# A decode block of attention and ReLU-gated MLP: in thirteen of fifteen steps the products of exponentials and V become a loop of two products per turn, with addresses in registers

## The chip, the cores and the metric

The kernel runs on one core of one Trainium2 chip. The metric is the device time of the program in microseconds (us): the median of 3 runs of the kernel before is 658.72 us (658.65 to 659.09). One further execution was taken by the hardware profiler; it took 658.71 us, of which 656.9 us lie between its first and its last instruction (the span). Times "at" a moment are counted from the start of that span.

## The reference, cut to what matters

One token of each of B = 2 batches passes a pre-norm attention block with a cached K and V, and then a gated MLP. 32 heads of 128 values each attend over 8192 cached positions; K and V together are 268 MB of bfloat16, and each byte is used once.

```python
h = x + _A_ref(_layernorm(x, axis=-1), A_k_cache, A_v_cache, A_wq, A_wo)
h2 = h + _B_ref(_layernorm(h, axis=-1), B_W_gate, B_W_up, B_W_down)
# in _A_ref, for one token (q: 1):
scores = jnp.einsum("bhqd,bhkd->bhqk", q, k) * (Dh ** -0.5)
p = _softmax(scores, axis=-1)
o = jnp.einsum("bhqk,bhkd->bhqd", p, v)
```

## The kernel before, in words

The 64 pairs of batch and head are taken four at a time: fifteen steps of four heads ("quads", i = 0 to 14), and the last quad as two halves. K of a quad is one transfer of 8.39 MB into a tile of 128 partitions by 32768 values: 32 partitions hold one head, and each partition holds 256 positions of 128 values. V of a quad has the same shape. Three such tiles (`bufs`) fill in turn: K of step i uses tile 2i mod 3, and V of step i uses tile 2i+1 mod 3. So V of step i+1 goes where K of step i was, and K of step i+2 goes where V of step i was. `load_tile` (L163 to L170) issues a transfer on SyncE's queue, SP, in one instruction (L168).

One step of the loop at L512 does the following.

- `scores_pe` (L515): the last 24 of the 256 positions of each partition (32 in step 0) go over TensorE. Transposes (L352), copies by ScalarE (L353), products with the query (L343) and some small steps put their scores into `scol`.
- `products` (L517, at L378) and `scores` (L523, at L396 and L398): VectorE multiplies the other 232 positions with the query and adds them up by halving. A last reduction (L402) gives the largest score of each partition.
- `largest_of_own` and `place_own` (L530, L533): a largest value is found for each head, ScalarE takes the exponentials (L418), and VectorE lays them out (L423) in `pgq`, the stationary operand of what follows: 64 blocks of 16 columns, one block for 4 positions.
- `values` (L443 to L454): 64 products on TensorE, one per block, each 128 x 16 against 128 x 512 of V, all added up in one bank of PSUM (`pv_ps`). They are 64 instruction pairs (load of weights, matmul) written out one after the other, with addresses fixed in the instructions. ScalarE copies the sum out (L454) to `pv`, to the rows that belong to the quad. In PSUM the sum stands on those same rows.
- After steps 3, 7 and 11 (and 14) the quads that are done are normalised together. So steps 4, 8 and 12 issue their first 8 products, then a small product for the sums (`sums`), and then the other 56.

Nothing here is ordered by a planner. The block at L190 (`tc.manual_schedule()`) keeps the order of the source on every engine, and semaphores are put in where one instruction needs another's result or its tile. A transfer stands in SP's queue where its `load_tile` stands in the source. In a step, V of the next step is asked for after `scores` (L527), and K of the step after next comes behind `values` (L547). Steps 12 and 13 deviate a little (L525, L542, L549, L551), because the last quad is split in two. What follows the loop (step 14, the two halves, the output projection and the MLP) is written out in the same manner.

Of the kernel before, what the change touches and what calls it, by code (L numbers as in the profile page):

```python
# [7 lines left out]
ACT = mybir.ActivationFunctionType  # L8
# [15 lines left out]
def kernel(  # L24
# [13 lines left out]
    nc = tc.nc  # L38
    P = nc.NUM_PARTITIONS
    B, Sq, D = A_x.shape  # L40
    _, Hkv, Sk, Dh = A_k_cache.shape
# [13 lines left out]
    HALF = TILE // 2  # L55
    TPC = 8
    VG = 4


    NPE = 32  # L60
# [37 lines left out]
    qpair = consts.tile([P, 2, Dh], bf16)  # L98
    pgq = consts.tile([P, TILE // Dh // VG, NH, VG], bf16)
    pgp = consts.tile([P, 2, HALF // Dh // VG, 2, VG], bf16)  # L100
    pv = consts.tile([P, VG * Dh], f32)
    pick = consts.tile([P, VG, 4, NH], f32)
    zc = consts.tile([P, B, NQ, NH], f32)
# [56 lines left out]
    steps = [Step(i) for i in range(LASTQ + 3)]  # L160
    Q = LASTQ

    def load_tile(cache, s, dst, pieces=1):  # L163
        h = NH * s.g + (0 if s.quad else 2 * s.k)
        n = s.nt * Dh
        w = n // pieces
        for k in range(pieces):
            nc.sync.dma_start(  # L168
                out=dst[:, k * w:(k + 1) * w], in_=_dram(cache, (s.b * Hkv + h) * Sk * Dh + k * w, [[n, P], [1, w]]),
            )  # L170
# [16 lines left out]
        nc.vector.reciprocal(out=rstd, in_=rstd)  # L187
        nc.vector.tensor_tensor(out=dst_bkc, in0=dev, in1=_free(rstd, 0, [[1, B], [0, KC]]), op=ALU.mult)

    with tc.manual_schedule():  # L190

        for b, k, n in ((0, 0, KC), (1, 0, KC)):
            nc.scalar.dma_start(
                out=xr[b:b + 1, k * P:(k + n) * P], in_=_dram(A_x, b * D + k * P, [[D, 1], [1, n * P]]),
# [10 lines left out]
            out=nscale, in_=nscale, compare_op=ALU.not_equal, fill=-SCALE,  # L205
# [5 lines left out]
            out=ident_f, in_=ident_f, compare_op=ALU.not_equal, fill=1.0,  # L211
# [4 lines left out]
            out=sel, in_=sel, compare_op=ALU.not_equal, fill=1.0,  # L216
# [9 lines left out]
            out=pick, in_=pick, compare_op=ALU.not_equal, fill=1.0,  # L226
# [24 lines left out]
        for g0 in range(0, NQ, 4):  # L251
            for n0 in range(NH * g0 * Dh, NH * (g0 + 4) * Dh, 4 * Dh):
                q_ps = ps2.tile([B, 4 * Dh], f32, tag="o")
                for c in range(KC):
                    nc.tensor.matmul(  # L255
                        out=q_ps, lhsT=xn[:, c, :], rhs=wq_sb[:, c, n0:n0 + 4 * Dh], start=(c == 0), stop=(c == KC - 1),
                    )
                nc.vector.tensor_copy(qrow[:, n0:n0 + 4 * Dh], q_ps)  # L258
            for b in range(B):
                r_ps = ps2.tile([P, 4, Dh], f32, tag="tp")  # L260
                for j in range(NH):
                    nc.tensor.matmul(
                        out=r_ps[j * (P // NH):(j + 1) * (P // NH)], lhsT=sel[:, b, 0:P // NH],
                        rhs=_free(qrow, (NH * g0 + j) * Dh, [[NH * Dh, 4], [1, Dh]]), start=True, stop=True,
# [4 lines left out]
        for j in range(2):  # L269
            nc.tensor.matmul(  # L270
                out=r_ps[j * (P // 2):(j + 1) * (P // 2)], lhsT=sel[:, B - 1, :],
                rhs=_free(qrow, (Hq - NH + j) * Dh, [[2 * Dh, 2], [1, Dh]]), start=True, stop=True,
            )
        nc.scalar.activation(out=qpair, in_=r_ps, func=ACT.Copy)
        for b in range(B):
# [3 lines left out]
            nc.vector.tensor_copy(  # L279
                qTs[:, b].rearrange("p (g j) -> p g j", j=NH), _free(qT_ps, 0, [[P, NQ], [P // NH, NH]]),  # L280
            )
        load_tile(A_k_cache, steps[1], steps[1].kt)

        nc.gpsimd.tensor_copy(
            qzp[:, :, 6:8], qTs[:, B - 1, Hq - NH:Hq].rearrange("p (k j) -> p k j", j=2),
        )
# [42 lines left out]
        def scores_pe(s, between=lambda: None):  # L329


            U = s.npe // 4
            nh, nv = s.nh, s.nv
            row_ps = ps.tile([nh * U, 4 * P], f32, tag="row")

            def times_q(c0):
                for k in range(0, TPC, 4):
                    u = (c0 + k) // 4
                    if s.quad:
                        z = qz[:, QZ - NH - NH * u:QZ - NH - NH * u + NH * U]  # L340
                    else:
                        z = qzp[:, s.k, 6 - 2 * u:6 - 2 * u + 2 * U]
                    nc.tensor.matmul(  # L343
                        out=row_ps, lhsT=z, rhs=s.kt[:, (nv + c0 + k) * Dh:(nv + c0 + k + 4) * Dh],
                        start=(u == 0), stop=(u == U - 1),
                    )

            for c0 in range(0, s.npe, TPC):
                t_ps = ps2.tile([P, TPC, P], bf16, tag="tp")
                for k in range(TPC):  # L350
                    t = nv + c0 + k
                    nc.tensor.transpose(t_ps[:, k, :], s.kt[:, t * Dh:(t + 1) * Dh], ident)  # L352
                nc.scalar.activation(  # L353
                    out=s.kt[:, (nv + c0) * Dh:(nv + c0 + TPC) * Dh], in_=t_ps.rearrange("p t s -> p (t s)"), func=ACT.Copy,
                )
                between()
                if c0:
                    times_q(c0 - TPC)
            times_q(s.npe - TPC)
            rows = s.kt[0:nh * U, nv * Dh:nv * Dh + 8 * P].bitcast(f32)  # L360
            nc.scalar.activation(out=rows, in_=row_ps, func=ACT.Copy)  # L361
            between()
            sc_ps = ps.tile([P, 4, U, nh], f32, tag="row", name="sc_ps")
            for t in range(4):
                nc.tensor.transpose(  # L365
                    sc_ps[:, t].rearrange("p u j -> p (u j)"), rows[:, t * P:(t + 1) * P], ident_f[0:nh * U, 0:nh * U],
                )
            for j in range(nh):
                r = s.rows(j)
                nc.scalar.activation(  # L370
                    out=scols[s.i][r, nv:s.nt].rearrange("p (u t) -> p t u", t=4), in_=sc_ps[r, :, :, j], func=ACT.Copy,
                )
# [67 lines left out]

        pv_ps = {}

        def values(s, u0, u1):  # L443

            r = slice(32 * (s.g % 4), 32 * (s.g % 4) + s.nh * VG)
            if u0 == 0:
                pv_ps[s.i] = ps2.tile([P, VG * Dh], f32, tag="o", name="pv_ps")
            for u in range(u0, u1):
                nc.tensor.matmul(  # L449
                    out=pv_ps[s.i][r, :], lhsT=s.pg[:, u].rearrange("p j t -> p (j t)"),  # L450
                    rhs=s.vt[:, u * VG * Dh:(u + 1) * VG * Dh], start=(u == 0), stop=(u == s.nt // VG - 1),
                )
            if u1 == s.nt // VG:
                nc.scalar.activation(out=pv[r, :], in_=pv_ps[s.i][r, :], func=ACT.Copy)  # L454

        def diagonals(i):

# [54 lines left out]
        for i in range(Q):  # L512
            s = steps[i]
            scols[i] = small.tile([P, s.nt], f32, tag="scol", name="scol")
            scores_pe(s)  # L515
            place_q(steps[i + 1])
            products(s)  # L517
            if i - 2 in groups:
                shares(i - 2)
                normalise(i - 2)  # L520
            if i == Q - 1:
                lay_rows(0, [spread(0, b) for b in range(B)], scalar=True)
            scores(s)  # L523
            if i == Q - 2:
                load_tile(A_k_cache, steps[Q], steps[Q].kt)  # L525
            else:
                load_tile(A_v_cache, steps[i + 1], steps[i + 1].vt)  # L527
            if i == Q - 1:
                scores_pe(steps[Q])
            largest_of_own(s)  # L530
            if i == Q - 1:
                products(steps[Q], 0, NEXT)
            place_own(s)  # L533
            half = s.nt // VG // 2
            ahead = 8 if i - 1 in groups else 0
            if ahead:
                own_sums(i - 1)
                values(s, 0, ahead)
                sums(i - 1)
            values(s, ahead, half)  # L540
            if i == Q - 1:
                load_tile(A_k_cache, steps[Q + 1], steps[Q + 1].kt)  # L542
            values(s, half, 2 * half)
            if i in groups:
                diagonals(i)
            if i + 2 < Q:
                load_tile(A_k_cache, steps[i + 2], steps[i + 2].kt)  # L547
            elif i == Q - 2:
                load_tile(A_v_cache, steps[Q - 1], steps[Q - 1].vt)  # L549
            else:  # L550
                load_tile(A_k_cache, steps[Q + 2], steps[Q + 2].kt)  # L551


        s, p0, p1 = steps[Q:]
# [16 lines left out]
        at = [0, 0]  # L571
# [28 lines left out]
        turns = iter((first, second, third))  # L600
# [3 lines left out]
        for w, src in ((0, B_W_gate), (1, B_W_up)):  # L604
            nc.sync.dma_start(
                out=wgu[:, w].rearrange("p c f -> p (c f)"), in_=_dram(src, 0, [[KC * F, P], [1, KC * F]]),
# [4 lines left out]
        f0, n = FSETS[-2]  # L611
        for d0 in range(0, D, D // 2):
            nc.sync.dma_start(
                out=wd_sb[:, f0 // P:f0 // P + n, d0:d0 + D // 2],
                in_=_dram(B_W_down, f0 * D + d0, [[n * D, P], [D, n], [1, D // 2]]),
# [9 lines left out]
            out=z2_ps, lhsT=ones, rhs=_free(zc, ((B - 1) * NQ + groups[Q][1]) * NH, [[1, nb]]), start=True, stop=True,  # L625
# [11 lines left out]
            out=parts3, in0=ident[0:PARTS, HI:HI + B], in1=ident[0:PARTS, LOW:LOW + B], op=ALU.add,  # L637
# [3 lines left out]
        half = p1.nt // 2  # L641
# [53 lines left out]
        for c in range(KC):  # L695
            nc.tensor.transpose(hT_ps[:, c, :], hb[:, c], ident)
        nc.scalar.activation(
            out=hrow.rearrange("q (p c) -> q p c", c=KC), in_=hT_ps.rearrange("q c p -> q p c"), func=ACT.Copy,
# [3 lines left out]
            out=shift, in0=_free(g_ps, ONE, [[ONE + 1, FC], [0, B]]), in1=_free(mean, 0, [[0, FC], [1, B]]), op=ALU.mult,  # L702
# [3 lines left out]
            out=gate, in_=_free(g_ps, 0, [[ONE + 1, FC], [1, B], [B, 2]]), axis=AXIS.X, op=ALU.add,  # L706
# [7 lines left out]
            out=gate, in0=gate, scalar=0.0, in1=_free(rvar, 0, [[0, FC], [1, B]]), op0=ALU.max, op1=ALU.mult,  # L714
# [63 lines left out]
```

## Time and profile before

| what | value |
|---|---|
| median of 3 runs | 658.72 us (658.65 to 659.09) |
| the profiled execution | 658.71 us; its span 656.9 us, so 1.8 us lie around the span |
| mean granted TensorE clock | 0.761 of full speed |
| VectorE busy | 557.1 us, 85% of the span |
| TensorE matmuls busy | 348.8 us, 53% |
| ScalarE busy | 123.6 us, 19% |
| products with V (L449), 960 in steps 0 to 14 | 239.7 us busy in sum |
| read from memory | 281.09 MB, 428 GB/s over the span |

An engine's busy time is the time in which the hardware profiler saw it work. Work on a semaphore, a branch or a register is not in it, and neither is the issuing of a transfer. A line of a group gives the busy time, the mean duration of one instruction, then the idle time before these instructions with what ended most of it. Matmuls are pipelined, so the mean duration of one (415 ns for L449) is longer than the distance between two (239.7 us by 960 is 250 ns). The chain of waits is followed back from the last instruction, at each step to what released it. In all views SPq is the queue of SP.

### The profile page before, as it was taken

To read this page: it belongs to the slowest core of one execution; us is meant where nothing else is said; L and a number is where in the kernel's file an instruction comes from. 1 tells how busy PE (TensorE), PEld (TensorE's weight loads), DVE (VectorE), ACT (ScalarE), POOL (GpSimd) and SP (SyncE) were. 2 spreads that over 40 slices of the span, in tenths; PEclk is the share of its full clock that TensorE was granted. 3 is DMA by queue.
4 is the path that set the end of the run, shared out by engine and by line. 5 is a ranking of instruction groups with operands and counts; after the bars stand their busy time and mean duration, and the time that the engine had idled before them with its cause. 6 is when DMAs were issued, how large, how long until landed. Compare 5 with 4: busy or idle time off the path is not lost.

```text
span 656.9 us, 5097 instructions
## 1 busy us (share of the span) xinstructions
PE 348.8 (53%) x2116; PEld 157.9 (24%) x2116; DVE 557.1 (85%) x248; ACT 123.6 (19%) x337; POOL 9.1 (1%) x37
## 2 busy tenths in 40 slices
PE   2530924709175380926538092562909458291997
PEld 1210311304022130312214031220403224130456
DVE  1399697988979799897979989797997969999982
ACT  1130030300203030030302103030210304201870
POOL 3000000000000000000000000000000000000020
PEclk9875876958778695877959588695957869576895
DMA  9999999999999999999999999999999999999997
GB/s 383 447 444 443 391 448 439 447 443 397 447 439 432 447 408 447 431 435 436 423 447 424 435 440 427 443 420 439 443 423 440 419 448 435 423 440 408 430 428 296
DMA packets 6766, 281.40 MB, mean 428 GB/s; under 512 B 724, under 2 KB 1368, under 8 KB 1624
## 3 DMA queue, kind: packets, MB, share of 16 engines
q1 hardware_dynamic: 6740, 281.09, 99.1%
q8 instruction: 16, 0.26, 0.1%
q14 instruction: 6, 0.05, 0.0%
q10 hardware_dynamic: 4, 0.00, 0.0%
HBM read 281.09 MB, written 0.00 MB: 428 GB/s over the span
## 4 chain that ended last, share of the span: by engine, by line
DVE 42%; DMA 40%; PE 16%; ACT 1%; issue 1%; SPq 0%; DVEq 0%; ACTq 0%
DMA tile<-in_A_k_cache_dram 31%; DVE tile L378 19%; DVE tile L396 18%; PE pv_ps L449 15%; DMA tile<-in_B_W_down_dram 4%; DMA tile<-in_A_wo_dram 4%; DVE scol L398 2%; DMA tile<-in_A_wq_dram 2%; PE q_ps L255 2%; DVE pgq L423 1%; ACT ecol L418 1%; DVE pm L402 0%; DVE qrep L398 0%; DVE pm L413 0%; DVE hmax L415 0%
## 5 line engine op out<-in xcount | busy, mean ns | idle before, releaser
L449 PE MATMUL pv_ps<-tile,pgq 128*16 128x512 bf16 x960 | 239.7, 415 | 239.9 <-DVE pgq L423 227.8
L378 DVE TENSOR_TENSOR tile<-tile,qrep 128x29696 bf16<-128x29696 bf16 (+3 forms) x16 | 232.4, 14524 | 49.0 <-DMA tile<-in_A_k_cache_dram 49.0
L396 DVE TENSOR_TENSOR tile<-tile 128x14848 bf16<-128x14848 bf16 (+7 forms) x68 | 236.4, 3477 | 2.2
L449 PEld LDWEIGHTS <-pgq 128*16 128x16 bf16 x960 | 90.7, 96 | 378.6 <-DVE pgq L423 238.5
L353 ACT ACTIVATE tile<-t_ps 128x1024 bf16<-128x1024 bf16 x53 | 52.6, 1022 | 17.4 <-PE t_ps L352 16.9
L454 ACT ACTIVATE pv<-pv_ps 16x512 f32<-16x512 f32 (+1 forms) x16 | 9.4, 588 | 238.9 <-PE pv_ps L449 238.8
L418 ACT ACTIVATE ecol<-scol,nmax 128x256 bf16<-128x256 f32 x14 | 7.1, 508 | 200.1 <-DVE nmax L417 200.1
L352 PE MATMUL t_ps<-ident,tile 128*128 128x128 bf16 x424 | 32.0, 227 | 17.5 <-DMA tile<-in_A_k_cache_dram 17.5
L343 PE MATMUL row_ps<-tile,qz 128*24 128x512 bf16 (+1 forms) x98 | 30.9, 398 | 17.9 <-ACT tile L353 17.8
L352 PEld LDWEIGHTS <-tile 128*128 128x128 bf16 x424 | 25.4, 102 | 32.7 <-DMA tile<-in_A_k_cache_dram 18.2
L398 DVE TENSOR_REDUCE scol<-tile 128x232 f32<-128x1856 bf16 (+1 forms) x14 | 28.9, 2067 | 0.5
L423 DVE TENSOR_TENSOR pgq<-ecol,ownb 128x1024 bf16<-128x1024 bf16 x15 | 10.4, 691 | 10.3 <-ACT ecol L418 10.3
L384 ACT ACTIVATE tile<-tile 128x128 bf16<-128x128 bf16 x60 | 17.6, 294 | 1.9 <-DVE tile L378 1.9
L378 DVE TENSOR_TENSOR tile<-tile,qpair 128x4096 bf16<-128x4096 bf16 (+3 forms) x4 | 15.5, 3881 | 0.0
L343 PEld LDWEIGHTS <-qz 128*24 128x24 bf16 (+1 forms) x98 | 7.9, 92 | 27.8 <-issue 22.7
L365 PE MATMUL sc_ps<-ident_f,tile 24*128 24x24 f32 (+2 forms) x68 | 7.4, 224 | 11.0 <-ACT tile L361 11.0
L370 ACT ACTIVATE scol<-sc_ps 32x24 f32<-32x24 f32 (+1 forms) x56 | 11.7, 209 | 7.7 <-PE sc_ps L365 7.2
L361 ACT ACTIVATE tile<-row_ps 24x512 f32<-24x512 f32 (+2 forms) x17 | 9.9, 585 | 14.0 <-PE row_ps L343 14.0
L258 DVE CAST tile<-q_ps 2x512 bf16<-2x512 f32 x8 | 5.4, 679 | 7.2 <-PE q_ps L255 7.2
L255 PE MATMUL q_ps<-tile,xn 128*2 128x512 bf16 x32 | 10.0, 477 | 2.5 <-DMA tile<-in_A_wq_dram 2.5
L384 ACT ACTIVATION_READ_ACCUMULATOR tile<-tile 128x1 f32 x60 | 11.2, 187 | 0.0
L365 PEld LDWEIGHTS sc_ps<-ident_f,tile 24*128 24x128 f32 (+2 forms) x68 | 5.6, 141 | 19.8 <-ACT tile L361 19.8
(135 smaller groups left out, 124.9 us busy)
## 6 DMA issues: line engine op xcount, KB each, us to landing
tile<-in_A_k_cache_dram SPq DMA_DIRECT2D x2, 4096.0 KB, 19.1
tile<-in_A_v_cache_dram SPq DMA_DIRECT2D x2, 4096.0 KB, 20.5
tile<-in_A_wq_dram SPq DMA_DIRECT2D x1, 4096.0 KB, 12.2
tile<-in_A_wo_dram SPq DMA_DIRECT2D x1, 2048.0 KB, 24.1
tile<-in_A_wo_dram SPq DMA_DIRECT2D x2, 1024.0 KB, 23.4
tile<-in_B_W_gate_dram SPq DMA_DIRECT2D x1, 1376.0 KB
tile<-in_B_W_up_dram SPq DMA_DIRECT2D x1, 1376.0 KB, 26.8
tile<-in_B_W_down_dram SPq DMA_DIRECT2D x1, 640.0 KB, 27.7
```

What stands on the lines that cost most here:

```text
L255: nc.tensor.matmul(out=q_ps, lhsT=xn[:, c, :], rhs=wq_sb[:, c, n0:n0 + 4 * Dh], start=(c == 0), stop=(c == KC - 1),)
L343: nc.tensor.matmul(out=row_ps, lhsT=z, rhs=s.kt[:, (nv + c0 + k) * Dh:(nv + c0 + k + 4) * Dh], start=(u == 0), stop=(u == U - 1),)
L352: nc.tensor.transpose(t_ps[:, k, :], s.kt[:, t * Dh:(t + 1) * Dh], ident)
L353: nc.scalar.activation(out=s.kt[:, (nv + c0) * Dh:(nv + c0 + TPC) * Dh], in_=t_ps.rearrange("p t s -> p (t s)"), func=ACT.Copy,)
L365: nc.tensor.transpose(sc_ps[:, t].rearrange("p u j -> p (u j)"), rows[:, t * P:(t + 1) * P], ident_f[0:nh * U, 0:nh * U],)
L378: nc.vector.tensor_tensor(out=kv, in0=kv, in1=_free(s.qr, 0, [[0, n], [1, Dh]]), op=ALU.mult)
L384: nc.scalar.activation(out=kv, in_=kv, func=ACT.Copy, accum_out=scols[s.i][:, t:t + 1])
L396: nc.vector.tensor_tensor(out=lo, in0=lo, in1=hi, op=ALU.add)
L398: nc.vector.tensor_reduce(out=scol[:, s.na:s.nv], in_=_free(s.kt, s.na * Dh, [[Dh, s.nv - s.na], [1, 8]]), axis=AXIS.X, op=ALU.add,)
L418: nc.scalar.activation(out=ecol, in_=scols[s.i], func=ACT.Exp, scale=SCALE, bias=nmax, accum_out=zs[:, s.b, s.g:s.g + 1],)
L423: nc.vector.tensor_tensor(out=s.pg, in0=_free(ecol, 0, [[VG, s.nt // VG], [0, NH], [1, VG]]), in1=_free(ownb, 0, [[0, s.nt // VG], [VG, NH ...
L449: nc.tensor.matmul(out=pv_ps[s.i][r, :], lhsT=s.pg[:, u].rearrange("p j t -> p (j t)"), rhs=s.vt[:, u * VG * Dh:(u + 1) * VG * Dh], start= ...
```

## The change

- In steps 0 to 12 `values` issues its products as a loop on TensorE (`Fori`). A first product, and a last one, stay ordinary instructions, since they open and close the sum. The 62 between them are 31 turns of two. In steps 4, 8 and 12 nine products come first, and 54 follow as 27 turns. Steps 13 and 14 and the halves keep the written-out form.
- A turn, as the changed kernel is built, holds two packed instructions of six register operations each (they work out the addresses of `pgq` and of V), two products that take their addresses from registers, one addition to the counter, and one compare-and-branch.
- The loop stands in a `tc.tile_critical()` block, and so the program is cut there into pieces. Every other engine gets one branch at each of the 13 places. TensorE gets, ahead of each loop, a series of semaphore waits and a branch, and behind it a branch, a semaphore increment, a drain and a wait before the last product. The waits ahead of loop i take in what the other engines and queues were given to do ahead of it; one of them is for K of step i+1 to have landed.
- The sum now stands on rows 0 to 15 of PSUM in every step, and ScalarE's copy puts it on the quad's rows of `pv`.
- In the source, K and V of the next step are both asked for behind `values`. In the built program SP's order of transfers is what it was: K of step i+1, branch of loop i, V of step i+1 (it waits for `scores` of step i), K of step i+2 (it waits for the last product of step i).
- GpSimd is no longer among the engines that keep the order of the source.

```diff
+    VU = 2
...
-    with tc.manual_schedule():
+    with tc.manual_schedule(engines={mybir.EngineType.PE, mybir.EngineType.DVE, mybir.EngineType.Activation, mybir.EngineType.SP}):
...
-        load_tile(A_k_cache, steps[1], steps[1].kt)
-
...
-        def values(s, u0, u1):
+        def values(s, u0, u1, looped=False):
...
+            out = pv_ps[s.i][0:n, :]
+            w = s.pg.rearrange("p u j t -> p (u j t)")
+
+            def step(u):
                 nc.tensor.matmul(
-                    out=pv_ps[s.i][r, :], lhsT=s.pg[:, u].rearrange("p j t -> p (j t)"),
-                    rhs=s.vt[:, u * VG * Dh:(u + 1) * VG * Dh], start=(u == 0), stop=(u == s.nt // VG - 1),
+                    out=out, lhsT=w[:, u * n:(u + 1) * n], rhs=s.vt[:, u * VG * Dh:(u + 1) * VG * Dh],
+                    start=(u == 0), stop=(u == s.nt // VG - 1),
                 )
+
+            def turns(u, v):
+                with tc.tile_critical(), nc.tensor.Fori(u * n, (v - VU) * n + 1, VU * n) as at:
+                    for k in range(VU):
+                        nc.tensor.matmul(
+                            out=out, lhsT=w[:, bass.ds(at + k * n, n)],
+                            rhs=s.vt[:, bass.ds(at * (VG * Dh // n) + k * VG * Dh, VG * Dh)],
+                            start=False, stop=False, skip_group_check=True,
+                        )
+
+            if looped:
+                lead = (s.nt // VG - 1 - max(u0, 1)) % VU + max(u0, 1)
+                for u in range(u0, lead):
+                    step(u)
+                turns(lead, s.nt // VG - 1)
+                step(s.nt // VG - 1)
+            else:
+                for u in range(u0, u1):
+                    step(u)
             if u1 == s.nt // VG:
-                nc.scalar.activation(out=pv[r, :], in_=pv_ps[s.i][r, :], func=ACT.Copy)
+                nc.scalar.activation(out=pv[r, :], in_=out, func=ACT.Copy)
...
+            if i < Q - 1:
+                values(s, ahead, whole, looped=True)
+                load_tile(A_k_cache, steps[i + 1], steps[i + 1].kt)
+                if i < Q - 2:
+                    load_tile(A_v_cache, steps[i + 1], steps[i + 1].vt)
+                else:
+                    load_tile(A_k_cache, steps[Q], steps[Q].kt)
+                    load_tile(A_v_cache, steps[Q - 1], steps[Q - 1].vt)
```

More of the change, by code (lines that the diff above doesn't have):

```diff
@@ L441 @@
         pv_ps = {}
-        def values(s, u0, u1):
+        def values(s, u0, u1, looped=False):
             r = slice(32 * (s.g % 4), 32 * (s.g % 4) + s.nh * VG)
+            n = s.nh * VG
             if u0 == 0:
                 pv_ps[s.i] = ps2.tile([P, VG * Dh], f32, tag="o", name="pv_ps")
-            for u in range(u0, u1):
+            out = pv_ps[s.i][0:n, :]
+            w = s.pg.rearrange("p u j t -> p (u j t)")
+            def step(u):
                 nc.tensor.matmul(
-                    out=pv_ps[s.i][r, :], lhsT=s.pg[:, u].rearrange("p j t -> p (j t)"),
-                    rhs=s.vt[:, u * VG * Dh:(u + 1) * VG * Dh], start=(u == 0), stop=(u == s.nt // VG - 1),
-                )
+                    out=out, lhsT=w[:, u * n:(u + 1) * n], rhs=s.vt[:, u * VG * Dh:(u + 1) * VG * Dh],
+                    start=(u == 0), stop=(u == s.nt // VG - 1),
+                )
+            def turns(u, v):
[15 more added lines that the diff above has]
+                    step(u)
             if u1 == s.nt // VG:
-                nc.scalar.activation(out=pv[r, :], in_=pv_ps[s.i][r, :], func=ACT.Copy)
+                nc.scalar.activation(out=pv[r, :], in_=out, func=ACT.Copy)
         def diagonals(i):
@@ L523 @@
             scores(s)
[L524 to L527, printed above, removed]
             if i == Q - 1:
+                load_tile(A_v_cache, steps[Q], steps[Q].vt)
                 scores_pe(steps[Q])
@@ L533 @@
             place_own(s)
-            half = s.nt // VG // 2
+            whole = s.nt // VG
+            half = whole // 2
             ahead = 8 if i - 1 in groups else 0
@@ L539 @@
                 sums(i - 1)
-            values(s, ahead, half)
-            if i == Q - 1:
+            if i < Q - 1:
[6 more added lines that the diff above has]
+                    load_tile(A_v_cache, steps[Q - 1], steps[Q - 1].vt)
+            else:
+                values(s, ahead, half)
                 load_tile(A_k_cache, steps[Q + 1], steps[Q + 1].kt)
-            values(s, half, 2 * half)
+                values(s, half, whole)
+                load_tile(A_k_cache, steps[Q + 2], steps[Q + 2].kt)
             if i in groups:
                 diagonals(i)
[L546 to L551, printed above, removed]
         s, p0, p1 = steps[Q:]
```

## The prediction

> **What bounds the kernel now.** I read the engines' busy times and the DMA queues first, then the chain of waits, then single steps in order of time.
>
> ```profile
> PE 348.8 (53%) x2116; PEld 157.9 (24%) x2116; DVE 557.1 (85%) x248; ACT 123.6 (19%) x337; POOL 9.1 (1%) x37
> q1 hardware_dynamic: 6740, 281.09, 99.1%
> HBM read 281.09 MB, written 0.00 MB: 428 GB/s over the span
> ```
>
> No engine is busy throughout, but the DMA queue is: its packets fill 99.1% of the 16 engines' time. The memory stream sets the end, and anything else costs time only if it leaves that stream empty. Whether it can is read from one period of the chain (columns: start, duration, what):
>
> ```profile
> 72.05 15.63 DVE tile L378
> ...
> 106.97 0.70 DVE pgq L423
> 107.72 15.38 PE pv_ps L449 x64
> 123.11 26.45 DMA tile<-in_A_k_cache_dram
> 149.59 15.64 DVE tile L378
> ```
>
> and from the same time by instruction (SPq is the issue of a transfer):
>
> ```profile
> 105.21 0.33 SPq L168 DMA_DIRECT2D tile<-in_A_v_cache_dram  x1
> 110.98 15.63 DVE L378 TENSOR_TENSOR tile<-tile,qrep 128x29696 bf16<-128x29696 bf16 x1 [3.32 <-DMA tile<-in_A_k_cache_dram]
> 123.11 0.33 SPq L168 DMA_DIRECT2D tile<-in_A_k_cache_dram  x1
> ```
>
> The times belong to steps 1 to 3. K of step 2 lands at 110.98, where VectorE, idle for 3.32 us, starts on it. K of step 3 lands at 149.59, 38.6 us later: two transfers of 8.39 MB, 19.3 us each. V of step 2 is queued at 105.21 and moves from 110.98 to about 130.3; K of step 3 is queued behind it at 123.11, when the last product of step 1 has read the tile. So K is asked for 12.1 us after the previous K landed. How late could it be? A transfer into an idle queue shows at the start:
>
> ```profile
> 0.73 12.19 DMA tile<-in_A_wq_dram
> ```
>
> 4.19 MB take 12.19 us from issue; at the rate above they are 9.65 us of moving, so 2.5 us are fixed. K may thus be asked for until 130.3 - 2.5 = 127.8, which is 16.8 us after the landing. The slack is 4.7 us a step, and beyond it each microsecond of delay is one of empty stream, since the next V waits in the same queue.
>
> **The change part by part.** *Removed*: 10 x 62 + 3 x 54 = 782 written-out pairs. On the engine they come back in the loop. What goes is fetching them: the two instruction queues move 0.31 MB in all, TensorE's 2116 pairs are most of that, so 782 of them are at most 0.11 MB, 0.3 us of the stream. I count nothing.
>
> *Moved*: no transfer changes its place in SP's queue (front). The branches of the other engines fall where these wait: SP between two transfers, ScalarE behind its exponentials, VectorE behind L423, with the 3.32 us idle behind it. At nothing; without that cover, about 0.06 us x 13 on VectorE.
>
> *Added wait*: loop i starts when K of step i+1 has landed, at 110.98 in the window, not at 107.72. Queued behind it on TensorE are the products and `scores_pe` of step 2, and whoever needs them: SP's K of step 3, and VectorE at L402 some 33 us after the landing. The wait moves the loop 3.3 us and eats that much of the slack. Then come entry and exit: at entry some semaphore waits, a register move and two branches, at exit a branch, an increment, a drain, a wait, and the last product (0.38 us). A sequencer's own instruction has a price in VectorE's rows:
>
> ```profile
> 102.98 2.09 DVE L398 TENSOR_REDUCE scol<-tile 128x232 f32<-128x1856 bf16 x1
> 105.17 0.42 DVE L402 TENSOR_REDUCE pm<-scol 128x1 f32<-128x256 f32 x1
> 105.62 0.21 DVE L413 STREAM_TRANSPOSE pm<-pm 128x32 f32<-128x32 f32 x1
> ```
>
> L402 has a semaphore instruction of its own ahead of it, and starts 0.10 us after L398; L413 has none and starts 0.03 us after L402. So one costs about 0.06 us. Entry is some 0.5 us, and exit 0.9 us with the array running empty: 1.4 us.
>
> *The loop* decides: 31 turns of t us. K is asked for 1.4 + 31t after the landing (27t in steps 4, 8 and 12), and the empty stream per step is 1.4 + 31t - 16.8.
>
> - From below: the array itself. Two products take 0.43 us at full clock (12.25 us for 56 in step 4, 0.22 each). About 1.7 us come on top at half clock, so 13.4 + 1.7 + 1.4 = 16.5 us: just inside 16.8. TensorE's sequencer passes an ordinary instruction in 18 ns:
>
> ```profile
> 647.13 1.59 PE L685 MATMUL g_ps<-tile,tile 128*128 128x5 bf16 x44 [0.49 <-DMA tile<-in_B_W_gate_dram]
> ```
>
> (44 pairs in 1.59 us). With the four other instructions at 0.06 us, a turn is 0.24 + 0.07 = 0.31 us, hidden under 0.43.
> - From above: each of the twelve packed operations costs as much as an instruction. 14 x 0.06 + 0.07 = 0.91 us.
> - Nearest row to a packed instruction: the issue of a transfer, which its sequencer also works out from many fields, 0.33 us (above). 2 x 0.33 + 2 x 0.06 + 0.07 = 0.85 us.
>
> The middle of 0.31 and 0.91 is 0.61; the nearest row says 0.85. I take 0.70 us, above the array's 0.43, so the sequencer becomes the bound of the loop. Per plain step 1.4 + 21.7 - 16.8 = 6.3 us, in the other three 1.4 + 18.9 - 16.8 = 3.5 us: 63 + 10.5 = 73.5 us. On the profiled execution's 658.71 us (its span and 1.8 around it; the median is 658.72) that is **732 us**. With t = 0.91 it is 128 + 27.5 = 155.5, so 814 us; with t at the array's 0.43 it stays 658.7.
>
> [...]
>
> **The rivals.**
>
> 1. *The loop hides: not slower.* If a packed instruction costs no more than about 0.08 us, t is at most 0.49, 31t + 1.4 stays within 16.8, and the stream never runs empty: **658.7 us**. For it: 4.7 us of slack, and 18 ns per ordinary instruction. Against: it leaves nothing for twelve register operations, and the start at half clock already takes what is left. Above t = 0.50 it ends. Chance 0.13.
>
> 2. *The clock falls back.* At 0.70 us a turn the array would be busy 61% of the time. In the windows (last columns: granted clock, DMA share, GB/s):
>
> ```profile
> 66.00:68.00 2.00, 1.06 (x3) 0.37 (x4) 0.69 (x1) 0.09 (x1) 0.00 (x0) 0.50 0.83 360
> 68.00:70.00 2.00, 2.00 (x7) 0.67 (x6) 0.00 (x0) 0.00 (x0) 0.00 (x0) 0.60 0.45 197
> 70.00:72.00 2.00, 2.00 (x11) 0.86 (x10) 0.00 (x0) 0.00 (x0) 0.00 (x0) 1.00 1.21 524
> ...
> 82.00:88.00 6.00, 3.90 (x35) 2.13 (x34) 5.97 (x2) 4.18 (x6) 0.00 (x0) 1.00 1.19 513
> ```
>
> the clock rises after some 3 us of products and is still 1.00 from 82 to 88, with the array busy 65%. If it fell to 0.50 in the loop, a product would take 0.43 us and a turn 0.86: 11.3 x 10 + 7.8 x 3 = 136 us, **795 us**. The row from 82 to 88 speaks against it. Chance 0.07. [...]
>
> 3. *A branch has to fetch its target.* A fetch from memory costs at least a transfer's fixed 2.5 us. Once per loop that is 13 x 2.5 = 32.5 us more: **764 us**. In every turn it is 31 x 2.5, or 77 us a loop, and about **1700 us**. For it: nothing in this trace, which has no loop. Against the second: a turn is a dozen instructions, and a fetch brings 16 KB (16 packets, 0.26 MB on the instruction queue). Chances 0.12 and 0.03. [...]
>
> **How the numbers follow.** Forecast, 732 us: 0.65. The rivals: 0.13, 0.07, 0.12 and 0.03. The range of 658 to 814 us takes in the hidden loop, the bounds of t, the clock and one fetch per loop; outside are a turn above 0.91 us and a fetch per turn, 0.15 to 0.2 in all. What can be told from no change is 0.2%, 1.3 us. Faster has only the 0.3 us of fetching: 0.02. Same is the hidden loop: 0.12. Slower: 0.86. The most likely cases alone span 690 to 790.
>
> **What would show it.** Right: DMA share gaps in each period, ended by K's issue; products of the loop at even distances of 0.3 to 0.45 us with the clock at 1.00, each pair apart by t; the first loop product a few tenths of a microsecond after VectorE's L378 starts; periods of 42 to 51 us instead of 38.6; SP waiting longer for the last product. Wrong: products at 0.22 us (rival 1), a clock of 0.50 in the loop (2), more instruction packets or a jump between turns (3), or a loop that starts before K lands, which would give 3.3 us of slack back.

## The result, and the profile after

The changed kernel takes 730.87 us (median of 4 runs, 730.74 to 731.09), the kernel before 658.75 us in the same comparison: slower by a ratio of 1.1094, 95% interval 1.1075 to 1.1113. The forecast was 732 us. Its profiled execution has a span of 728.9 us, against 656.9.

From the page of the changed kernel, the lines that answer to the first three of before:

```profile
PE 410.3 (56%) x2116; PEld 157.4 (22%) x2116; DVE 557.4 (76%) x248; ACT 123.4 (17%) x337; POOL 8.0 (1%) x37
q1 hardware_dynamic: 6740, 281.09, 90.5%
q8 instruction: 11, 0.18, 0.1%
HBM read 281.09 MB, written 0.00 MB: 386 GB/s over the span
```

VectorE and ScalarE do the same work as before. The same bytes move, but the queue that was full for 99.1% of the span is now full for 90.5%. Nothing was added to the stream; it has holes. Share times span is the time that the packets themselves took: 651.0 us before, 659.7 us after. So some 63 of the 72 us are empty queue, and in the other 9 the same packets took longer (where, is shown below). The instruction queue moved 11 packets of 16 KB; before, it moved 16.

One period in order of time (columns: start, duration, engine and line, in brackets the idle time before it and its releaser):

```profile
107.90 0.59 PE L452 MATMUL pv_ps<-tile,pgq 128*16 128x512 bf16 x1 [7.61 <-DVE pgq L422]
116.52 15.63 DVE L377 TENSOR_TENSOR tile<-tile,qrep 128x29696 bf16<-128x29696 bf16 x1 [8.68 <-DMA tile<-in_A_k_cache_dram]
117.08 21.18 PE L460 MATMUL pv_ps<-tile,pgq 128*16 x62 [8.59 <-DMA tile<-in_A_k_cache_dram]
138.46 0.38 PE L452 MATMUL pv_ps<-tile,pgq 128*16 128x512 bf16 x1 [0.20 <-PEq L458]
138.86 0.33 SPq L169 DMA_DIRECT2D tile<-in_A_k_cache_dram  x1
161.48 15.63 DVE L377 TENSOR_TENSOR tile<-tile,qrep 128x29696 bf16<-128x29696 bf16 x1 [9.35 <-DMA tile<-in_A_k_cache_dram]
```

A landing is read here as the start of VectorE's L377, which waits for it. The first product of step 1 runs at 107.90, when its exponentials are laid out. The 62 of the loop wait until K of step 2 has landed at 116.52, start 0.56 us later, and last 21.18 us, where 64 took 15.38 before. So K of step 3 is asked for 22.34 us after the landing of K of step 2 (before: 12.13) and lands 22.62 us after that. One landing follows the other by 44.96 us, against 38.6. In the windows of the same stretch (last columns: clock, DMA share, GB/s) the hole can be seen:

```profile
118.00:120.00 2.00, 2.00 (x6) 0.54 (x5) 2.00 (x1) 0.00 (x0) 0.00 (x0) 0.50 0.98 426
122.00:124.00 2.00, 2.00 (x10) 0.68 (x8) 2.00 (x1) 0.00 (x0) 0.00 (x0) 0.97 1.21 524
...
134.00:136.00 2.00, 1.73 (x7) 0.51 (x6) 2.00 (x1) 0.00 (x0) 0.00 (x0) 1.00 0.00 0
136.00:138.00 2.00, 1.73 (x7) 0.51 (x6) 2.00 (x1) 0.00 (x0) 0.00 (x0) 1.00 0.00 0
138.00:140.00 2.00, 1.64 (x19) 1.07 (x18) 2.00 (x1) 1.11 (x2) 0.00 (x0) 1.00 0.88 295
```

The view counts a packet whole in the window in which it starts, so a share can be above 1. At 524 GB/s 16 packets of 64 KB start in 2 us, and a share of 1.21 gives each 2.42 us. The last packets of V of step 2 start before 134 and by their records end at 135.6; the first of K, asked for at 138.86, start at 139.8. In between the queue is empty. The nine packets in the last row take 3.1 us each, by the same working. In the whole trace 209 packets of 64 KB take over 2.6 us, against 18 before. Nearly all of them are the first sixteen or so of a K asked for late, and together they make up the 9 us; why such packets take longer, no run tells.

TensorE is not busy throughout: from 124 to 138, at a granted clock of 1.00, its products fill 1.73 to 1.78 us of each 2. The idle 0.42 to 0.47 us ahead of a turn's weight loads are put down to `issue`, so to no wait that the profile shows; they are read here as waiting for TensorE's own sequencer, which narrow_products and narrow_fixed_addresses below test. The loads of three turns show the pace:

```profile
123.95 0.24 PEld L460 LDWEIGHTS pv_ps<-tile,pgq 128*16 x2 [0.42 <-issue]
124.62 0.24 PEld L460 LDWEIGHTS pv_ps<-tile,pgq 128*16 x2 [0.43 <-issue]
125.33 0.24 PEld L460 LDWEIGHTS pv_ps<-tile,pgq 128*16 x2 [0.47 <-issue]
```

From 123.95 to 137.66 us these are 20 turns, 0.686 us each. What the sequencer does in them shows in the records of the loop's two lines on TensorE's queue, PEldq (count, then minimum, median and maximum in ns; 391 is the number of turns):

```profile
L458 PEldq FUSED_REGOPS  x391: 78/78/83, 72.6 to 623.6; - x196
L458 PEldq ALU_OP  x391: 36/36/39, 73.0 to 623.9; - x196
L458 PEldq COMPARE_BRANCH  x391: 76/208/227, 73.1 to 624.0; - x196
...
L460 PEldq FUSED_REGOPS  x391: 74/74/74, 72.7 to 623.8; - x196
```

Per turn: two packed instructions of 78 and 74 ns, an addition of 36 ns, and a branch of 208 ns. Of the 391 branches 13 are of 76 ns, as many as there are loops, and no other is below 207 ns; so 76 ns is taken to be the last branch of a loop, which does not jump back. That is 0.396 us of the 0.686 us of a turn; the other 0.290 us lies between the records, which do not show what it is made of.

Over the 12 periods from the landing of K of step 1 to that of step 13 the kernel before takes 537.39 - 72.05 = 465.3 us, and the changed one 605.10 - 72.23 = 532.9: 67.5 us of the 72.0 by which the spans differ. The last loop, in step 12, delays V of step 13, asked for 19.9 us after that landing instead of 12.0, and the stretch from there to the end is 4.3 us longer.

The chain of waits is of little use here. Followed back from the end it breaks off after some 104 us, at the product behind the last loop. Periods and landings still can be read.

### The profile page after: what moved, and what is told of

Same layout as the page of the kernel before. It is cut to its first block, busy times and chain, and to the rows that moved or that the text cites. A ratio compares the mean times of both kernels' runs of the same rounds, so it can differ in the third digit from the quotient of the medians.

```text
span 728.9 us, 6857 instructions
## 1 busy us (share of the span) xinstructions
PE 410.3 (56%) x2116; PEld 157.4 (22%) x2116; DVE 557.4 (76%) x248; ACT 123.4 (17%) x337; POOL 8.0 (1%) x37
## 3 DMA queue, kind: packets, MB, share of 16 engines
q1 hardware_dynamic: 6740, 281.09, 90.5%
## 5 line engine op out<-in xcount | busy, mean ns | idle before, releaser
L377 DVE TENSOR_TENSOR tile<-tile,qrep 128x29696 bf16<-128x29696 bf16 (+3 forms) x16 | 232.4, 14525 | 117.6 <-DMA tile<-in_A_k_cache_dram 117.6
L460 PE MATMUL pv_ps<-tile,pgq 128*16 x782 | 242.6, 421 | 128.5 <-issue 59.2
L460 PEld LDWEIGHTS pv_ps<-tile,pgq 128*16 x782 | 71.5, 91 | 301.3 <-issue 272.3
L452 PE MATMUL pv_ps<-tile,pgq 128*16 128x512 bf16 x178 | 55.4, 451 | 119.9 <-DVE pgq L422 109.5
L452 PEld LDWEIGHTS <-pgq 128*16 128x16 bf16 x178 | 17.1, 99 | 149.2 <-DVE pgq L422 113.3
L351 PE MATMUL t_ps<-ident,tile 128*128 128x128 bf16 x424 | 33.7, 234 | 19.6 <-DMA tile<-in_A_k_cache_dram 19.6
L342 PE MATMUL row_ps<-tile,qz 128*24 128x512 bf16 (+1 forms) x98 | 32.2, 413 | 17.8 <-ACT tile L352 17.7
L351 PEld LDWEIGHTS <-tile 128*128 128x128 bf16 x424 | 26.9, 105 | 33.6 <-DMA tile<-in_A_k_cache_dram 20.3
L377 DVE TENSOR_TENSOR tile<-tile,qpair 128x4096 bf16<-128x4096 bf16 (+3 forms) x4 | 15.5, 3885 | 1.3 <-DMA tile<-in_A_k_cache_dram 1.3
```

The source lines that it names most:

```text
L342: nc.tensor.matmul(out=row_ps, lhsT=z, rhs=s.kt[:, (nv + c0 + k) * Dh:(nv + c0 + k + 4) * Dh], start=(u == 0), stop=(u == U - 1),)
L377: nc.vector.tensor_tensor(out=kv, in0=kv, in1=_free(s.qr, 0, [[0, n], [1, Dh]]), op=ALU.mult)
L452: nc.tensor.matmul(out=out, lhsT=w[:, u * n:(u + 1) * n], rhs=s.vt[:, u * VG * Dh:(u + 1) * VG * Dh], start=(u == 0), stop=(u == s.nt // V ...
L460: nc.tensor.matmul(out=out, lhsT=w[:, bass.ds(at + k * n, n)], rhs=s.vt[:, bass.ds(at * (VG * Dh // n) + k * VG * Dh, VG * Dh)], start=Fal ...
```

## The experiments

The theory: the sequencer, not the array, sets the pace of the loop; together with the wait this makes K's issue late, and from a deadline on each microsecond is one of empty stream. The rivals: the wait or the cut of the program costs the time by itself; the array or its clock bounds the loop; the branch, not the packed instructions, is what is dear. In what follows x is the time from one landing of K to the issue of the next K, as a mean over steps that don't begin with eight products ahead; before it is 12.5, in the changed kernel 22.65 us. It is read from the one profiled execution of each run. Where the executions of a run spread, that one need not stand for the median: cut_alone's is its fastest, turns_of_four's its slowest.

**wait_alone**: cut and wait, but no loop.

```diff
-                with tc.tile_critical(), nc.tensor.Fori(u * n, (v - VU) * n + 1, VU * n) as at:
-                    for k in range(VU):
...
+                with tc.tile_critical():
+                    for k in range(u, v):
```

> The cut and the wait stay (each of the 13 places, with the wait for K of the next step), but the 62 (54) products between first and last are written out with fixed addresses instead of a loop. Theory (the turns of the loop cost the time, since they push the issue of K past the slack): products at 0.22 us once the clock is up, K asked for about 16 us after the landing of the K before, the stream runs empty hardly at all: 659 us, at most 664. Rival (cut, wait, entry and exit cost it by themselves): well over 690 us, up to 731.

Measured: 671.16 us (668.86 to 672.07), ratio 1.0178 (1.0158 to 1.0197). Neither of the two: the turns cost most of it, but what is left is not free. In its trace:

```profile
112.23 16.20 PE L460 MATMUL pv_ps<-tile,pgq 128*16 128x512 bf16 x62 [3.74 <-DMA tile<-in_A_k_cache_dram]
128.63 0.38 PE L452 MATMUL pv_ps<-tile,pgq 128*16 128x512 bf16 x1 [0.20 <-PEq L458]
```

62 products take 16.20 us. At a clock of 1.00 one follows the other by 0.216 us (in step 4 of the kernel before 56 take 12.25 us, the last of them 0.38), which makes 13.4. The other 2.8, not 1.7, are lost at the start, where the granted clock is 0.50 until 117 and 0.84 from 117 to 119. x is 16.96 (16.3 to 17.8), right at the deadline, and the landings lie 39.7 us apart. The queue is full for 98.3% of a span of 668.3 us. So of the 11.4 us by which this span is longer, only about half are empty queue; in the rest packets took longer, as in the changed kernel (140 of them over 2.6 us).

**no_wait_for_k**: the loop stays, the wait goes. An edge for the issue order alone, without a semaphore, puts SP's K of step i+1 behind loop i.

```diff
                 load_tile(A_k_cache, steps[i + 1], steps[i + 1].kt)
+                behind(last_load[0], last_step[0])
```

> The loop of two products per turn stays; K of step i+1 stands behind loop i in SP's program, so that loop i no longer waits for it. SP's order of transfers and what each transfer waits for stay. Theory: the loop starts about 36.4 us after its own K has landed, takes 21.2 us, and K of the step after next lands 0.6 + 22.6 us later: 80.8 us for two steps instead of 77.2, 1.8 us a step, 24 us in all: 683 us (676 to 692). Rival (the wait alone costs it): 659 us. Rival (the wait costs nothing, the turns cost all): 731 us.

Measured: 687.5 us, ratio 1.0432 (1.0417 to 1.0447), inside the theory's range. x is 18.6, against 22.65 with the wait. The loop starts once its exponentials are there and is as long as ever:

```profile
108.20 0.59 PE L455 MATMUL pv_ps<-tile,pgq 128*16 128x512 bf16 x1 [11.74 <-DVE pgq L425]
110.04 21.20 PE L463 MATMUL pv_ps<-tile,pgq 128*16 x62 [1.24 <-issue]
```

**cut_alone**: neither loop nor wait (both edits above).

> Neither loop nor wait for K: the products are written out with fixed addresses, only the cut of the program at the 13 places remains (branches on every engine, entry, exit, and the sum on rows 0 to 15). Theory (entry and exit cost TensorE some 2 us a step, which the slack takes for the most part): K asked for 13.5 to 15 us after the landing, 659 to 663 us. Rival (the cut is dear by itself, and what wait_alone lost was its): 668 to 673 us, as wait_alone.

Measured: 663.91 us (661.52 to 666.88), ratio 1.0093 (1.0057 to 1.0129). A little dearer than expected, although x, 14.5, is as expected. Behind its first product TensorE pauses for about 1.0 us at the entry, and the 62 products behind it take 16.49 us, again with a slow start: the first nine take 4.01 us, where 0.216 us from one to the next would make 2.1:

```profile
107.82 0.59 PE L455 MATMUL pv_ps<-tile,pgq 128*16 128x512 bf16 x1 [16.40 <-DVE pgq L425]
109.44 16.49 PE L463 MATMUL pv_ps<-tile,pgq 128*16 128x512 bf16 x62 [1.02 <-PEq L461]
```

Not the price of wait_alone, so the rival falls, but the slack does not take all of it. And here the loss is no hole in the stream:

```profile
q1 hardware_dynamic: 6740, 281.09, 99.1%
```

The queue is as full as before, and the span of the profiled execution is 2.5 us longer (659.4 against 656.9). The packets took that much longer: 68 of them over 2.6 us, 23 of these between 128 and 133, behind the K with the largest x, 15.9, which landed 1.7 us late.

Cut alone costs 5 us, with the wait 12, with the loop 28, with both 72. The wait costs 7 us beside written-out products and 44 us beside the loop. Of two delays one behind the other, the first uses up the slack. Beside the loop the wait is paid in full: it moves x by 4.1 us, and the landings lie 4.1 us further apart (44.9 against 40.8).

**turns_of_one and turns_of_four** (`VU = 1`, `VU = 4`) take the turn apart.

> As the changed kernel, with one product per turn (62 turns, 54 in steps 4, 8 and 12). Theory, with the prices of the prediction: 0.41 us a turn, about 787 us. Rival (dear branch): 0.55 us a turn, about 897 us.

> As the changed kernel, with four products per turn (15 turns, 13 in steps 4, 8 and 12). Theory, with the prices of the prediction (0.26 us for a packed instruction, 0.12 for addition and branch): a turn of 1.28 us, K asked for 20.4 us after the landing, 708 us. Rival (the taken branch is dear, 0.4 us, the packed instructions cheap, 0.1 us): 0.95 us a turn, nearly the array's own 0.86, 660 us.

Measured: 874.54 us (one run) and 673.77 us (669.02 to 675.76; ratio 1.0212, 1.0175 to 1.0249). The prices of the prediction fail in both; the rival comes near in the first and lies 14 us too low in the second. The weight loads of single turns, with one product and with four:

```profile
128.51 0.09 PEld L460 LDWEIGHTS pv_ps<-tile,pgq 128*16 x1 [13.35 <-issue]
129.03 0.09 PEld L460 LDWEIGHTS pv_ps<-tile,pgq 128*16 x1 [0.43 <-issue]
```

```profile
124.83 0.58 PEld L460 LDWEIGHTS pv_ps<-tile,pgq 128*16 x4 [0.28 <-issue]
125.84 0.54 PEld L460 LDWEIGHTS pv_ps<-tile,pgq 128*16 x4 [0.43 <-issue]
```

0.525 us (mean of ten) for one product, 0.686 for two, 0.995 for four (mean of two): some 0.16 us per product and 0.36 us per turn. So the rival's turn of 0.95 us was about right, but its 660 us were too few. By its prices x would have been 15.7 (1.4 + 15 x 0.95), inside the deadline and so free; x is 16.7, at the deadline as in wait_alone.

**turns_of_eight**, and **no_wait_turns_of_eight** with the edit of no_wait_for_k.

> As the changed kernel, with eight products per turn (7 turns behind 7 written-out products). From the runs with one, two and four products per turn (0.523, 0.683 and 0.995 us) a turn costs 0.36 us and each product in it 0.16 us. Theory by that line: 1.64 us of the sequencer per turn, less than the 1.73 us that the array takes for eight products, so the loop goes at 0.216 us a product, K is asked for 16.3 to 17.8 us after the landing as with written-out products behind the wait, and the time is that of wait_alone, 667 to 673 us. Rival (the price grows with the size of a turn): above 680 us.

> Eight products per turn and no wait for K of the next step. Theory (both causes are gone, entry and exit alone remain, some 2 us a step inside the slack): K asked for about 15 us after the landing of the K before, 659 to 662 us. Rival (the cut of the program costs something by itself): above 664 us.

Measured: 668.46 us (ratio 1.0151, 1.0134 to 1.0168) and 664.69 us (ratio 1.0095, 1.0076 to 1.0113), just above the edge of the rival. The first time is as expected, but x is not: 15.1 on average, where 16.3 to 17.8 were expected. With eight a turn, seven written-out products instead of one run before the wait, and the expectation did not count that. That the time came out right all the same is in part luck, since steps inside the deadline also lose a little. The second is the same as cut_alone within its interval: with eight products a turn no cost of the loop itself is left to be seen, and the cut remains. Its x spreads from 12.9 to 16.6.

**narrow_products** and **narrow_fixed_addresses**: is it the array or the sequencer, and what in the sequencer?

```diff
-                            out=out, lhsT=w[:, bass.ds(at + k * n, n)],
-                            rhs=s.vt[:, bass.ds(at * (VG * Dh // n) + k * VG * Dh, VG * Dh)],
+                            out=out[:, 0:Dh // 2], lhsT=w[:, (u + k) * n:(u + k + 1) * n],
+                            rhs=s.vt[:, (u + k) * VG * Dh:(u + k) * VG * Dh + Dh // 2],
```

(narrow_products keeps `bass.ds` in both operands.)

> As the changed kernel, but each product of the loop takes 64 of the 512 columns, so it leaves out most of the sums; the turns and their register operations stay. Theory (the sequencer bounds the loop): the turn stays at 0.68 us, and the time at about 731 us. Rival (the array, at whatever clock, bounds it): the turn falls towards 0.1 us, time 659 us.

> As narrow_products, but both products of a turn always use the same block, by fixed addresses, so the sums are left out; the packed instructions are gone, the addition to the counter, the branch and two narrow products stay. Theory (0.36 us a turn for counter and branch, 0.16 a product of which about 0.12 is the packed instruction): 0.43 us a turn. With the prices of the prediction (0.12 us for counter and branch, 0.26 for a packed instruction) it would be 0.19 us. The time: 659 to 662 us either way.

Measured: 733.23 and 659.14 us (one run each). A turn with an eighth of the columns, and then the same without packed instructions:

```profile
117.57 0.37 PE L460 MATMUL pv_ps<-tile,pgq 128*16 x2 [8.92 <-DMA tile<-in_A_k_cache_dram]
118.24 0.37 PE L460 MATMUL pv_ps<-tile,pgq 128*16 x2 [0.31 <-issue]
118.91 0.40 PE L460 MATMUL pv_ps<-tile,pgq 128*16 x2 [0.30 <-issue]
```

```profile
112.08 0.10 PEld L460 LDWEIGHTS pv_ps<-tile,pgq 128*16 128x16 bf16 x2 [0.28 <-issue]
112.47 0.10 PEld L460 LDWEIGHTS pv_ps<-tile,pgq 128*16 128x16 bf16 x2 [0.28 <-issue]
112.85 0.10 PEld L460 LDWEIGHTS pv_ps<-tile,pgq 128*16 128x16 bf16 x2 [0.28 <-issue]
```

The windows of the first of these loops (clock in the third column from the right):

```profile
121.00:123.00 2.00, 1.10 (x6) 0.52 (x6) 2.00 (x1) 0.00 (x0) 0.00 (x0) 0.50 0.60 262
135.00:137.00 2.00, 1.09 (x7) 0.52 (x6) 2.00 (x1) 0.00 (x0) 0.00 (x0) 0.50 0.00 0
```

The turn of narrow products keeps its 0.67 to 0.72 us, although the granted clock is 0.50 in all five windows read of that loop, from 117 to 137. So neither array nor clock bounds it. Without packed instructions 0.388 us are left (mean of twenty; 0.43 expected), and x falls to 13.6. The two packed instructions thus cost 0.686 - 0.388 = 0.298 us a turn, 0.15 us each with what they hold up.

**narrow_v_by_register** takes five of the twelve register operations out, **narrow_fixed_four** puts four products by fixed addresses into a turn.

> As narrow_products, but the stationary operand of both products of a turn is always the same block, by a fixed address, so most sums are left out; V's address stays in a register, and the two packed instructions shrink from six operations each to four and three. Between 0.683 us (twelve operations) and 0.383 us (no packed instruction) a turn: if the operations are what costs, about 0.56 us; if the instruction costs by itself, whatever it holds, above 0.63 us.

> As narrow_fixed_addresses, with four narrow products per turn, always the same blocks. If counter and branch are what the 0.383 us of that turn consist of, two further pairs of load and product at some 0.02 to 0.04 us each leave 0.42 to 0.46 us a turn; if the products were the bound there, 0.77 us.

Measured: 715.78 and 659.28 us (one run each).

```profile
L460 PEldq FUSED_REGOPS  x391: 46/46/46, 73.2 to 608.4; - x196
```

```profile
111.99 0.21 PEld L460 LDWEIGHTS pv_ps<-tile,pgq 128*16 128x16 bf16 x4 [0.22 <-issue]
112.38 0.21 PEld L460 LDWEIGHTS pv_ps<-tile,pgq 128*16 128x16 bf16 x4 [0.17 <-issue]
112.76 0.20 PEld L460 LDWEIGHTS pv_ps<-tile,pgq 128*16 128x16 bf16 x4 [0.17 <-issue]
```

With seven operations instead of twelve a turn takes 0.638 us (mean of 14): some 9 ns an operation, so by this estimate about 0.1 of a packed instruction's 0.15 us does not go with the number of its operations. The second packed instruction's own record agrees: 46 ns for three operations, 74 for six. Two more pairs by fixed addresses cost nothing, 0.388 us as with two (0.42 to 0.46 expected). So 0.39 us is what the way round costs, addition and taken branch: 0.244 us of records and about 0.14 us that no record covers. Whether the sequencer waits there for its next instructions, no run tells; the turn's length without branch was not tried.

## Why the prediction was right, by its steps

- **The bound**, a stream that costs only where it runs empty: confirmed for the bulk. The DMA queue's share fell to 90.5%, and the holes stand where the working put them, between the end of V and the late issue of K. But some 9 of the 72 us are the slow first packets of each late K, which the prediction has no term for.
- **The deadline**, K asked for at the latest 16.8 us after the landing, with a transfer into an idle queue at 21.8 us: in the changed kernel it takes 22.3 us on average from issue to landing, so 16.3. The edge is also soft. Steps with x from 14 to 16 already lose some tenths of a microsecond in cut_alone and no_wait_turns_of_eight, and near 16 up to 1.7 us. In cut_alone slow packets set in although the queue is full for 99.1% of the span. Counted as free up to the edge, these losses were missed.
- **The wait and the entry**: the loop starts 0.56 us after the landing (0.5 predicted), and x less 31 turns is about 1.4 us (22.65 - 31 x 0.686), as predicted.
- **The turn**, 0.70 us predicted, 0.686 measured. Per plain step 44.94 us from landing to landing (44.9 predicted: 38.6 + 6.3), 41.7 us in the steps with eight products ahead (42.1). That 44.94 meets 44.9 so closely is luck: x was predicted 0.45 us too long (23.1 against 22.65), and the transfer behind it about as much too short (21.8 against 22.3).
- **How the 0.70 was made up was wrong.** The price of counter and branch was taken as 0.12 us, twice a semaphore instruction; they cost 0.39 us. The rest went to the packed instructions, 0.26 us each; they cost 0.15. For two products a turn the errors cancel. That the sum came out right is luck too: 0.70 was a choice between 0.61 and 0.85, and its parts were off by a factor of three one way and almost two the other. For one product a turn they gave 787 us against 874.54, for four 708 against 673.77. The row taken as nearest to a packed instruction, a transfer's 0.33 us, is about twice its price; that the two are alike was the author's analogy, and no run shows what the 0.33 us are spent on.
- **The array's floor**, "just inside" the deadline: not quite. The slow start costs 2.8 us in wait_alone and, by the same sum, 3.1 in cut_alone, and wait_alone lost 12 us where the working had nothing. One product and a pause stand ahead of the 62 there; that they are why the start is so long is not shown.
- **Removed fetching**: five 16 KB packets fewer, 0.08 MB (at most 0.11 predicted), nothing to be seen in the time.
- **Rival 1**, a hidden loop, needs at most 0.08 us for a packed instruction and less than 0.5 us a turn: they cost 0.15 and 0.686. **Rival 2**, the clock: granted at 1.00 from 124 until the loop ends. **Rival 3**, a fetch: fewer packets, the longest branch took 227 ns where a fetch was priced at 2.5 us (the author's estimate, from the fixed part of a transfer), and the 1.4 us of entry and exit leave no room for one per loop. (A turn is eight instructions, not a dozen.)

## What to carry to other kernels

Before an instruction stream is turned into a loop, compare the sequencer's time for a turn with the array's. Here the way round cost 0.39 us and the address work of each product 0.15 us, against 0.216 us that the array takes for a product. By that sum, an estimate, a turn needs six or seven products for the loop to hide; eight was the next size tried, and it hid. Where a stream of transfers is the bound, note for each transfer how late it may be asked for; two delays share that slack, and together they can cost far more than the sum of both (here 7 and 23 us beyond the cut alone, and 67 together). A total that comes out right does not confirm its parts: vary the count of one part.

## What was not expected of the hardware

- A branch back to the start of the loop records 208 ns on TensorE's queue (the median of 391 in the changed kernel), and a turn without address work takes 0.388 us, whether it holds two narrow products (narrow_fixed_addresses) or four (narrow_fixed_four).
- A packed register instruction with three to six operations cost about 0.1 us plus 9 ns per operation here, an estimate from turns of 0.388, 0.638 and 0.686 us (narrow_fixed_addresses, narrow_v_by_register, the changed kernel).
- A turn's time did not follow the array's clock: 0.67 to 0.72 us in narrow_products at a granted 0.50, 0.686 us in the changed kernel at 1.00.
- In turns_of_four x is 16 to 17.5 us, so K's 8.39 MB are asked for some 2 to 3 us before the queue would run empty (19.3 us after the landing). They did not land on a sharp schedule: landings followed each other by 38.7 to 41.7 us.
- Time was lost while the queue never looked empty: in cut_alone it is full for 99.1% of the span, as before, while the packets took 2.5 us longer. In the changed kernel the first packets of each late K took some 3.1 us instead of 2.42.
